# Fused attention and gated FFN on one core: another order of the opening, with the row sums of the first tiles folded before TensorE adds them

## The chip, the cores and the metric

The kernel runs on one core of a Trainium2 chip. The metric is the time of one execution in device microseconds (us); the median of three runs before the change is 1024.46 (1024.46 to 1024.63). Engines are named as in the profile: PE is TensorE, DVE is VectorE, ACT is ScalarE, POOL is GpSimd, SP is SyncE, which here only issues DMAs.

## What is computed

```python
B, C, Hh, Ww = 4, 128, 384, 32             # N = Hh*Ww = 12288 rows of q per image
kv_pool = kv.reshape(B, H//4, 4, W//4, 4, C).mean(axis=(2, 4))
k = v = kv_pool.reshape(B, -1, C) @ w_sr    # 768 keys per image
s = (q @ k.transpose(0, 2, 1)) / sqrt(C)
a = exp(s - s.max(-1)); a /= a.sum(-1)
x = (a @ v).reshape(B * N, C)               # 49152 rows
out = (maximum(x @ w_gate, 0) * (x @ w_val)) @ w_out    # d_ff = 1536
```

## The kernel before

The rows of q are cut into 96 tiles of 512. For a tile k the kernel makes the scores against 768 keys (six chunks of 128), exponentials, the product with the values (x, channels by rows), then twelve blocks of the FFN: v (value projection, L504), y (copy of v's bank to f16, L510), g (gate projection, L516), h (relu of the gate times the value, on DVE, L523), o (output projection, accumulated over the twelve, L545). The softmax's division is put off: the output is multiplied by the square of the inverse row sum, since the FFN is homogeneous of degree two in x.

Tiles 6 to 95 are worked by a loop over the fixed list STEADY (L106), one pass for each tile, in which four tiles overlap: scores of k, values of k-2, v, y, g, h of k-3, o of k-4. There ACT makes the exponentials with their row sums, and the weights' rows come transposed by DMA.

The change lies ahead of that loop, in the opening. A list of words, OPENING (L75), is walked once from left to right (L812); `open_step` (L678) issues for each word the instructions of one step. Every engine runs its instructions in the order in which they were issued, so the list is the order of each engine's queue; which engine takes a copy or an add is looked up by the word in ENGINES (L66: v DVE, a ACT, p POOL). "@n" names the PSUM bank (0 to 7) that the step's tile gets; the step then waits until the bank's last reader is done. Semaphores carry only dependences of data and of buffers.

The words, with the lines behind them:

- The twelve lines of the first image's kv (three pairs of chunks, four lines of pixels each, 512 KB a line, L229) and the first four tiles of q are loaded by SP and ACT (L641 to L646). Lines 0 to 3 of a pair hold the four rows of a 4x4 pooling window, for both chunks of the pair.
- a, b, c: adds of two lines, or of a line to the sum (L274); SUMS (L112) names the lines. p: sum of pixels 0, 1 with 2, 3 (L279); r: the last two pixels (L687). All are 128x512, 128x256, 128x128 in f32.
- T: transposes on PE, accumulated in one bank of chunk j: of a raw line (four pixels, four matmuls), or of a pixel sum ("p" two, "r" one) (L293). A raw line is thus added by PE instead of by an add. kvT: copy out of the bank; pj: product with w_sr; key: scaled copy to f16; vt, val: the same transposed, as values.
- cast, qt, qT: a tile of q to f16, its transpose on PE, the copy out of the bank. Tiles 4 and 5 come later: ql (L187) loads them, cast4 and cast5 run on POOL, qT4 and qT5 are DMA transposes on SP (L214).
- S k.j, E k.j, V k.j: scores, exponentials, values of tile k (0 to 3) and chunk j (L374, L380, L451). In these four tiles keys lie on the partitions, so ACT can't sum rows. xT k: copy of x out of its bank.
- U j...: the row sums of the four tiles over the chunks named: for each chunk four matmuls with 32 columns of ones, side by side in the array (L467). R: the sums transposed by DVE (L482); R2: inverse and square (L488); lsc: sixteen small copies of them on POOL (L493), used in the output of tiles 0 to 3.
- D, F: matmuls whose result nobody reads (L736, L670). The two of `fill(2)` (L667) stand ahead of the list.
- gate, W, wo, qd, qn, k: a tiny POOL copy that waits for a line of kv, then DMAs by POOL of the weights, and of q for later tiles.
- s, e of tiles 4 and 5, and oT (output transposed on DVE, scaled on POOL), as in the steady list.

Of the kernel before, what the change touches and what calls it, by code (L numbers as in the profile page):

```python
# [16 lines left out]
def kernel(  # L17
# [120 lines left out]
    def copy_on(name, to, what):
        engine = engine_of(name)
        if engine is nc.scalar:  # L140
            nc.scalar.copy(to, what)  # L141
        else:
# [765 lines left out]
```

## Time and profile before

| | us |
|---|---|
| median of three runs | 1024.46 |
| span of the profiled execution | 1022.5 |
| PE busy | 1017.2 |
| ACT busy | 918.5 |
| DVE busy | 869.4 |
| POOL busy | 524.0 |
| first v of the opening on PE | 27.74 |
| first word of the steady list on PE (v10 of tile 3) | 53.00 |

The span runs from the profiled execution's first instruction to its last; its own time as a run is not listed apart, and the runs' median lies 2.0 us above the span. Times in the timeline count from the span's start. A row of the timeline gives start, length and count of instructions merged into it; what stands in brackets is how long the engine was idle before, and whose end released it. A matmul's row includes the time that its result takes through the array, which overlaps the next one.

### The profile page before, as it was taken

The page shows a single profiled execution, that of the slowest core. Times are in us where ns is not written, and L with a number is a line of the kernel's source. Part 1 is how long each engine was busy: PE and PEld are TensorE (multiplying, and loading weights), DVE is VectorE, ACT ScalarE, POOL GpSimd, SP SyncE. Part 2 cuts the span into 40 slices and gives each one's busy share as a digit, 9 for nine tenths or more (in the row PEclk, how much of TensorE's full clock was granted, in tenths as well). Part 3 has the DMA queues.
Part 4 walks back from the last instruction along what each step waited for, and adds up shares of the span by engine and source line. Part 5 has one row for each costly group of instructions (what it writes and reads, how often), then busy time and mean ns, then how long its engine had stood idle before and what let it go on. Part 6 is the DMA issues. An engine that isn't in the chain of part 4 may idle for free.

```text
span 1022.5 us, 17480 instructions
## 1 busy us (share of the span) xinstructions
PE 1017.2 (99%) x5021; PEld 485.2 (47%) x5021; DVE 869.4 (85%) x1450; ACT 918.5 (90%) x1927; POOL 524.0 (51%) x1312
## 2 busy tenths in 40 slices
PE   9999999999999999999999999999999999999998
PEld 4444444444444444444444444444444444444445
DVE  5988888888888888888888888888888888888888
ACT  5999998999999999999999999999999999999986
POOL 3487857344437576544434856754434543443342
PEclk9999999999999999999999999999999999999999
DMA  9999999878799999868779999978787878777651
GB/s 317 172 171 184 186 211 145 140 122 132 132 198 156 201 164 184 136 116 143 125 134 201 165 186 187 157 131 137 128 130 114 147 122 129 124 119 124 98 91 44
DMA packets 475743, 153.48 MB, mean 150 GB/s; under 512 B 451584, under 2 KB 465920, under 8 KB 475648
## 3 DMA queue, kind: packets, MB, share of 16 engines
q1 hardware_dynamic: 453184, 126.08, 65.9%
q0 software_dynamic: 22032, 25.19, 17.6%
q10 hardware_dynamic: 432, 1.11, 0.3%
q8 instruction: 39, 0.64, 0.3%
q14 instruction: 56, 0.46, 0.2%
HBM read 53.94 MB, written 26.35 MB: 79 GB/s over the span
## 4 chain that ended last, share of the span: by engine, by line
PE 99%; DMA 1%; DVE 0%; ACTq 0%; issue 0%
PE bank_ps L504 24%; PE bank_ps L515 24%; PE bank_ps L545 24%; PE wide_ps L397 12%; PE bank_ps L439 12%; PE bank_ps L529 1%; DMA kv_in<-in_kv_dram 1%; PE bank_ps L456 1%; PE bank_ps L378 1%; PE wide_ps L336 0%; PE bank_ps L300 0%; PE bank_ps L314 0%; PE bank_ps L474 0%; DVE kv_s L272 0%; PE bank_ps L209 0%; ACTq L246 0%
## 5 line engine op out<-in xcount | busy, mean ns | idle before, releaser
L523 DVE SCALAR_TENSOR_TENSOR hT<-bank_ps,val 128x512 f16<-128x512 f32 x1152 | 727.3, 679 | 104.4 <-PE bank_ps L515 83.7
L141 ACT CAST val<-bank_ps 128x512 f16<-128x512 f32 x1149 | 628.4, 596 | 44.4 <-PE bank_ps L504 23.9
L504 PE MATMUL bank_ps<-xT,wv 128*128 128x512 f16 x1152 | 421.0, 379 | 0.0
L515 PE MATMUL bank_ps<-xT,wg 128*128 128x512 f16 x1152 | 376.3, 379 | 0.0
L545 PE MATMUL bank_ps<-hT,wo 128*128 128x512 f16 x1116 | 348.7, 379 | 0.0
L402 ACT ACTIVATE a<-wide_ps 128x768 f16<-128x768 f32 x368 | 302.2, 821 | 44.0 <-PE wide_ps L397 44.0
L397 PE MATMUL wide_ps<-kv,qT 128*128 128x512 f16 x736 | 179.8, 326 | 0.0
L439 PE MATMUL bank_ps<-aT,kv 128*128 128x512 f16 x552 | 179.0, 379 | 0.0
L558 POOL TENSOR_TENSOR o_sb<-o_t,scale 128x512 f32<-128x512 f32 x89 | 93.2, 1047 | 158.8 <-issue 141.0
L545 PEld LDWEIGHTS <-wo 128*128 128x128 f16 x1116 | 109.1, 98 | 132.1 <-issue 0.5
L515 PEld LDWEIGHTS <-wg 128*128 128x128 f16 x1152 | 112.6, 98 | 122.5 <-issue 0.2
L504 PEld LDWEIGHTS <-wv 128*128 128x128 f16 x1152 | 112.5, 98 | 105.4 <-issue 0.4
L423 POOL COPY scale<-square 32x8 f32<-32x8 f32 x736 | 141.2, 192 | 28.6
L416 POOL TENSOR_TENSOR square<-inverse 128x8 f32<-128x8 f32 x46 | 9.3, 202 | 248.9 <-DVE inverse L414 248.9
L838 POOL DMA_DIRECT2D out_dram<-o_sb x208 | 130.3, 632 | 9.6 <-POOL o_sb L558 7.4
L397 PEld LDWEIGHTS <-qT 128*128 128x128 f16 x736 | 71.9, 98 | 87.0 <-issue 0.2
L447 DVE CAST xT<-bank_ps 128x512 f16<-128x512 f32 x92 | 63.6, 691 | 31.7 <-PE bank_ps L439 31.6
L439 PEld LDWEIGHTS <-kv 128*128 128x128 f16 x552 | 53.9, 98 | 65.2
L402 ACT ACTIVATION_READ_ACCUMULATOR a<-wide_ps 128x1 f32 x368 | 76.1, 207 | 0.0
L553 DVE STREAM_TRANSPOSE o_t<-bank_ps 128x512 f32<-128x512 f32 x93 | 65.4, 703 | 0.3 <-PE bank_ps L504 0.2
L162 POOL DMA_DIRECT2D q<-in_q_dram x84 | 48.8, 581 | 0.3 <-issue 0.3
L256 POOL TENSOR_TENSOR s<-kv_in 128x512 f32<-128x512 f32 x36 | 45.1, 1281 | 0.7
(86 smaller groups left out, 210.8 us busy)
## 6 DMA issues: line engine op xcount, KB each, us to landing
kv_in<-in_kv_dram SPq DMA_DIRECT2D x42, 512.0 KB, 5.3
out_dram<-o_sb SPq DMA_DIRECT2D x177, 64.0 KB, 3.6
q<-in_q_dram POOLq DMA_DIRECT2D x88, 128.0 KB, 3.4
out_dram<-o_sb POOLq DMA_DIRECT2D x176, 64.0 KB, 4.2
aT<-a SPq DMA_TRANSPOSE x184, 4.5
kv_line<-in_kv_dram SPq DMA_DIRECT2D x4, 512.0 KB, 9.8
placed<-blocks SPq DMA_DIRECT2D x9, 128.0 KB, 2.5
kvT<-placed SPq DMA_DIRECT2D x36, 32.0 KB, 2.2
```

The source lines that it names most:

```text
L141: nc.scalar.copy(to, what)
L397: nc.tensor.matmul(s_ps[:, j0 * 128 : j1 * 128], qT, kv16[:, b, j0:j1, 0:C], start=True, stop=True)
L402: nc.scalar.activation(a16s[k][:, s, :], s_banks.pop(s)[:, 0:J], AF.Exp, scale=qk_scale, accum_out=a_sums[k // 2][:, k % 2, s : s + 1],)
L423: nc.gpsimd.tensor_copy(to[32 * b : 32 * (b + 1), :, :, j], squares[k // 2][32 * j : 32 * (j + 1)])
L439: nc.tensor.matmul(x_banks[k], kv16[:, k // NST, jc, C : 2 * C], aT[:, jc], start=first, stop=x_left[k] == 0,)
L504: nc.tensor.matmul(proj_banks["v", k, fb], wv16[:, fb * 128 : (fb + 1) * 128], xTs[k], start=True, stop=True,)
L515: nc.tensor.matmul(proj_banks["g", k, fb], wg16[:, fb * 128 : (fb + 1) * 128], xTs[k], start=True, stop=True,)
L523: nc.vector.scalar_tensor_tensor(hTs[k][:, fb, :], freed(proj_banks.pop(("g", k, fb))), 0.0, vals.pop((k, fb)), op0=ALU.max, op1=ALU.mult,)
L545: nc.tensor.matmul(o_banks[k], wo16[:, fb, :], hTs[k][:, fb, :], start=first, stop=o_left[k] == 0)
L553: nc.vector.transpose(o_t, freed(o_banks.pop(k)))
L558: nc.gpsimd.tensor_tensor(to, o_by, scale.to_broadcast([128, NS, 4, 32]), op=ALU.mult)
L838: queue.dma_start(*out_moves.pop())
```

## The change

- Each of the first six chunks now takes two line adds (lines 0 and 1, then 2), one pixel sum and one raw line: T j.3 and T j.p. Before, chunks 0, 2 and 5 turned two raw lines each, and chunks 1, 3 and 4 none.
- The row sums: new words m k.n add the exponentials of chunks 2n and 2n+1 of tile k, n k.1.2 adds the third sum to the second, so that chunks 0 and 1 lie in one f16 tile, chunks 2 to 5 in another. U6.7 then is the only sums step, over these two. Of the twelve m five are on DVE and seven on POOL; the four n are on POOL.
- D0, F384 and F256 go; D1 stays, in another place. `fill(2)` stays.
- The list and the engines are written anew. The gate of the weight loads waits for the same line (4.1 is line 1 of chunk 4), but stands behind m1.0 and m0.0 on POOL.
- The loads are named by a list; it gives the two queues the same transfers in the same order as before.

```diff
+    LOADS = """
+        p0l1:a p0l0 p0l3:a p0l2 w Q0 Q2 p1l0 p1l1 p1l2 p1l3 p2l0 p2l1 p2l2 p2l3
+    """.split()
-    SUMS = [{"a": [1, 0]}, {"a": [1, 0], "b": ["s", 3], "c": ["s", 2]}, {"a": [0, 1]}, {"a": [0, 1], "b": ["s", 2], "c": ["s", 3]}, {"a": [0, 1], "b": ["s", 2], "c": ["s", 3]}, {"a": [0, 1]}]
+    SUMS = [
+        {"a": [0, 1], "b": ["s", 2]},
...
+    ]
+    def pair_of(k, n):
+        if n not in a_pairs:
+            a_pairs[n] = work.tile(
+                [128, LEAD, T], FP16, tag="kv_s2" if n else "a_pair", bufs=2 if n else 1, name="a_pair"
+            )
+        return a_pairs[n][:, k]
+    def add_chunks(name, k, n):
+        add(name, pair_of(k, n), aTs[k][:, 2 * n], aTs[k][:, 2 * n + 1])
+    def add_pairs(name, k, n, m):
+        add(name, pair_of(k, n), pair_of(k, n), pair_of(k, m))
```

The engines and the list, before (-) and after (+), up to the first score blocks:

```diff
-        a0:v a1:v p0:v r0:v b1:v c1:v p1:v kvT0:v r1:p cast0:a cast1:a key0:v kvT1:v qT0:v
-        cast2:a cast3:v qT1:v val0:v key1:v qT2:v qT3:v val1:a a2:v a3:v p2:p b3:v c3:v kvT2:a
-        p3:p key2:a kvT3:a val2:v a5:v key3:v p5:v a4:v r5:v b4:v val3:a c4:v kvT5:a p4:v key5:v
-        kvT4:a val5:v key4:v val4:v xT0:v xT2:v y0.8:v y0.2:a xT1:v y2.0:a y0.10:a cast4:p y0.7:a
+        cast1:a a1:v a0:p b1:p b0:v cast0:a p0:v p1:p kvT0:a cast3:v kvT1:a qT1:v key0:v cast2:v
+        key1:v qT3:v qT0:a qT2:v val1:v a2:v val0:v b2:v p2:v a3:p kvT2:a b3:v p3:v kvT3:v key2:v
+        m3.0:v key3:v val2:v a5:v b5:v p5:v a4:v kvT5:a b4:v val3:a p4:v m1.0:p key5:v m0.0:p
+        m1.1:v m3.1:v kvT4:a val5:v key4:a m0.1:v val4:v m0.2:v xT0:v xT2:v xT1:v y0.10:a y0.2:a
+        y0.8:v y0.0:a y0.7:a y0.4:a m2.1:p m2.2:p y2.0:a m2.0:p m1.2:p y0.6:a cast4:p n2.1.2:p
+        y0.1:a cast5:p n0.1.2:p xT3:a y2.1:a y1.8:a y1.0:a m3.2:p n1.1.2:p y1.10:a y0.9:a n3.1.2:p
...
-        D1@2 D0@2 F384@2 a0 a1 p0 r0 T0.r@0 T0.3 b1 T0.2 c1 F256@2 p1 kvT0 r1 cast0 pj0@0 T1.r@1
-        cast1 qt0@2 key0 kvT1 vt0@0 qT0 qt1@3 cast2 pj1@1 cast3 S0.0@2 qT1 qt2@4 E0.0 qt3@5 val0
-        key1 qT3 S1.0@3 E1.0 vt1@1 val1 V0.0@2 S1.1@0 E1.1 S0.1@5 E0.1 qT2 S2.0@4 S2.1@1 V1.0@3
-        a2 S3.1@6 V1.1 E3.1 V0.1 S3.0@5 T2.2@0 V3.1@6 p2 E2.1 a3 T2.p V2.1@1 E2.0 b3 T2.3 c3 E3.0
-        U0.1@5 kvT2 pj2@0 V2.0 key2 p3 T3.p@4 kvT3 S2.2@0 E2.2 vt2@7 val2 V3.0 gate2.1 S1.2@4
-        E1.2 pj3@7 a5 S0.2@0 V2.2 W0 key3 W1 ql4 ql5 S3.2@4 E0.2 E3.2 p5 V1.2 a4 S3.3@7 S0.3@0
-        E3.3 V0.2 T5.2@4 E0.3 r5 T5.r vt3@7 val3 T5.3 kvT5 wo S1.3@0 S2.3@7 b4 c4 p4 V3.3 pj5@4
-        V3.2 E1.3 T4.p@0 E2.3 V1.3 key5 vt5@4 S2.5@7 kvT4 val5 pj4@0 key4 E2.5 S0.5@4 E0.5 V0.3
-        V2.3 S0.4@0 vt4@7 E0.4 V2.5 val4 S1.4@4 V0.5 E1.4 S2.4@7 V0.4 xT0 E2.4 S1.5@0 E1.5 S3.5@4
-        V1.4 V2.4 E3.5 S3.4@7 qd3 xT2 v0.8@2 v0.2@0 E3.4 qd1 V1.5 y0.8 v0.10@4 y0.2 v2.0@1 qd0
-        U2.3.4.5 xT1 y2.0 qd2 y0.10 cast4 v0.7@3 R v0.6@1 y0.7 g0.2@4 qT4 g2.0@0 h0.2 v0.0@2 y0.6
-        v2.1@3 cast5 g0.7@5 h2.0 V3.5 y0.0 g0.6@4 v0.1@1 qT5 h0.7 V3.4 y2.1 v1.10@2 g0.10@0 h0.6
-        xT3 o0.7@5 g0.1@3 y0.1 o0.2 h0.10 o0.6 y1.10 v0.5@4 h0.1 g0.0@1 g2.1@0 y0.5 v0.4@2 h0.0
-        o0.10 y0.4 v0.3@3 g0.4@4 h2.1 o0.0 y0.3 g1.10@2 v0.9@1 h0.4 g0.5@0 y0.9 v1.8@3 h1.10 s4.0
+        T0.3@2 cast1 a1 a0 b1 b0 cast0 T1.3@5 p0 p1 D1@6 T0.p kvT0 cast3 qt1@0 T1.p kvT1 qt0@3
+        pj0@1 qT1 key0 qt3@4 pj1@2 cast2 key1 S1.0@6 qt2@5 qT3 S1.1@7 S3.1@1 qT0 S3.0@0 qT2 vt1@3
+        vt0@2 S2.1@4 E1.0 val1 E1.1 S0.0@6 a2 E3.1 S2.0@5 V3.1@7 V1.1@1 S0.1@3 E2.1 val0 b2 E3.0
+        V1.0 p2 E2.0 V2.1@2 a3 V3.0 V2.0 T2.p@4 E0.0 E0.1 T2.3 kvT2 T3.3@0 b3 p3 T3.p pj2@5 kvT3
+        key2 m3.0 V0.0@6 pj3@3 S1.2@0 V0.1 vt2@4 key3 val2 E1.2 S3.2@5 a5 S2.2@3 S0.3@4 b5 p5 V1.2
+        S0.2@0 E3.2 E2.2 V3.2 E0.2 S1.3@5 V2.2 E1.3 S3.3@3 V0.2 E3.3 a4 T5.p@0 T5.3 vt3@3 kvT5
+        S2.3@5 pj5@0 b4 val3 T4.3@3 E0.3 p4 m1.0 T4.p key5 m0.0 m1.1 m3.1 S2.5@4 E2.3 kvT4 vt5@0
+        S0.5@5 val5 gate4.1 E2.5 pj4@3 W0 V3.3 V2.3 key4 m0.1 V2.5 E0.5 W1 ql4 S0.4@3 vt4@0 S2.4@4
+        ql5 S1.5@5 val4 E0.4 E2.4 V0.5 wo S1.4@0 V0.3 E1.5 E1.4 V0.4 S3.4@3 qd1 qd2 m0.2 V2.4
+        S3.5@4 V1.5 V1.3 E3.4 V1.4 E3.5 xT0 v0.10@5 v0.8@6 xT2 v0.2@0 g0.10@3 xT1 y0.10 y0.2 g0.2@2
+        v0.0@4 v2.0@1 qd3 v0.7@5 g0.7@0 y0.8 qd0 h0.10 v0.4@6 y0.0 V3.4 g0.0@4 y0.7 v0.6@3 h0.2
+        y0.4 g2.0@5 V3.5 g0.6@2 m2.1 h0.7 v0.1@6 m2.2 y2.0 h0.0 m2.0 v2.1@0 m1.2 g0.1@1 v1.8@4 y0.6
+        o0.7@3 cast4 n2.1.2 h2.0 o0.0 y0.1 v1.10@6 cast5 n0.1.2 xT3 g0.4@5 h0.6 g2.1@7 v1.0@2 y2.1
+        o0.10 y1.8 y1.0 o0.2 g1.8@0 h0.1 h0.4 m3.2 v0.9@1 qT4 g0.5@4 h2.1 n1.1.2 y1.10 y0.9 h1.8
+        v0.5@5 g1.10@2 qT5 s4.0 o0.4 v0.3@1 o0.1 g0.9@0 n3.1.2 h1.10 o0.6 v1.11@2 y0.5 e4.0 g0.8@5
+        h0.5 y0.3 s4.1 y1.11 U6.7@4 h0.9 h0.8 v1.1@1 e4.1 R g0.3@0 v2.3@2 o0.9 y1.1 h0.3 y2.3
...
```

More of the change, by code (lines that the diff above doesn't have):

```diff
@@ L471, in lead_sums @@
                 x_banks["sums"] = bank([128, T])
-            sums_left[0] -= 1
             for k in range(LEAD):
                 nc.tensor.matmul(
-                    x_banks["sums"][32 * k : 32 * (k + 1), :], ones, aTs[k][:, jc, :],
-                    start=first, stop=sums_left[0] == 0, skip_group_check=True,
+                    x_banks["sums"][32 * k : 32 * (k + 1), :], ones,
+                    aTs[k][:, jc, :] if jc < NJC else pair_of(k, jc - NJC),
+                    start=first, stop=last and jc == chunks[-1], skip_group_check=True,
                     tile_position=(0, 32 * k),
```

86 lines of the change are left out of this document (54 added, 32 removed).

## The prediction, made before the changed kernel was run

> **What bounds the kernel now.** I read the page first (totals, then the chain that ended last), then busy time by windows, then the timeline of the first 56 us, engine by engine. The text names steps by the words of the order lists: E2.5 is tile 2's exponential over chunk 5, S, V, T, v, y, g, h, o, U, m, n likewise, k.x meaning tile k.
>
> ```profile
> span 1022.5 us, 17480 instructions
> PE 1017.2 (99%) x5021; PEld 485.2 (47%) x5021; DVE 869.4 (85%) x1450; ACT 918.5 (90%) x1927; POOL 524.0 (51%) x1312
> ...
> PE 99%; DMA 1%; DVE 0%; ACTq 0%; issue 0%
> ```
>
> TensorE is the chain to the end. The edit touches only the opening list, so the question is when the first word of the steady list (v10, the 37th value projection) reaches TensorE; everything behind it keeps its length, if the engines hand over in the same state.
>
> ```profile
> 27.74 0.59 PE L504 MATMUL bank_ps<-xT,wv 128*128 128x512 f16 x2
> ...
> 28.91 1.05 PE L474 MATMUL bank_ps<-aT,ones 128*32 128x512 f16 x16
> ...
> 36.17 0.49 PE L397 MATMUL wide_ps<-kv,qT 128*128 128x512 f16 x2
> ...
> 53.00 0.38 PE L504 MATMUL bank_ps<-xT,wv 128*128 128x512 f16 x1
> ```
>
> The opening's first projection starts at 27.74, the steady list at 53.00. In the chain of waits a projection counts for what it adds, not for its row's 0.38:
>
> ```profile
> 27.91 0.43 PE bank_ps L504 x2
> ```
>
> That is 0.216 each; a score block (the 0.49 of 36.17, less the same tail of 0.16) adds 0.33. The profiled execution's time is the span 1022.5 plus 2.0 around it, which is the median 1024.46; so a change of the 53.00 goes straight into the median.
>
> ```profile
> 5.00:8.50 3.50, 3.37 (x8) 1.17 (x7) 1.94 (x5) 0.00 (x0) 0.00 (x0) 1.00 1.03 415
> ...
> 12.40:27.70 15.30, 15.30 (x97) 8.14 (x95) 10.02 (x23) 13.27 (x30) 7.46 (x14) 1.00 1.06 302
> ...
> 30.70:53.00 22.30, 22.30 (x108) 10.32 (x106) 22.18 (x40) 21.55 (x47) 12.11 (x34) 1.00 0.94 161
> ```
>
> Columns: stretch, length, busy time of PE, PEld, DVE, ACT, POOL, granted clock, DMA share, GB/s. Until 12.4 DMA is full and the engines wait for data. From 12.4 to 27.7 ACT is the fullest engine (24 exponentials and copies). From 30.7 to 53 PE, DVE (22.18 of 22.30) and ACT (21.55) are all full: a balanced stage, in which none of the three has room.
>
> **Part 1, loads.** The new load list gives each queue the same transfers in the same order; cost nothing. This fixes the end of the exponentials:
>
> ```profile
> 19.22 0.19 POOL L747 COPY gate<-kv_line 128x1 f32<-128x1 f32 x1 [0.96 <-DMA kv_line<-in_kv_dram]
> ...
> 21.28 0.42 PEld L300 LDWEIGHTS bank_ps<-ident,kv_line 128*128 128x128 f32 x4 [0.33 <-ACT aT L381]
> ...
> 22.59 0.27 ACT L141 COPY kvT_chunk<-bank_ps 128x128 f32<-128x128 f32 x1 [0.18 <-PE bank_ps L300]
> ...
> 23.98 0.27 ACT L141 COPY kvT_chunk<-bank_ps 128x128 f32<-128x128 f32 x1
> ...
> 24.41 4.32 ACT L381 ACTIVATE aT<-bank_ps 128x512 f16<-128x512 f32 x8 [0.17 <-PE bank_ps L378]
> ...
> 28.58 3.54 ACT L141 CAST val<-bank_ps 128x512 f16<-128x512 f32 x6
> ```
>
> POOL's gate waits for line 1 of the last pair, 19.2. Two more lines of 512 KB at the 415 GB/s of the first window (1.26 us each) come at 20.5 and 21.7 by estimate. The eight exponentials of chunks 4 and 5 (0.52 us each with their gaps, 24.41 to 28.58) can't start until the last line is transposed, copied, projected and kept. No order of the list moves that by more than some tenths.
>
> **Part 2, the start.** Chunks 0 and 1 now take two line adds each (a1, b0 on DVE, a0, b1 on POOL), a pixel sum and one raw line, and the fillers go. What sets the first exponential is not the sums but the copies of q:
>
> ```profile
> 10.23 1.90 ACT L141 CAST q<-q 128x512 f16<-128x512 f32 x3 [6.57 <-DMA q<-in_q_dram]
> ...
> 11.89 0.42 DVE L143 CAST q<-q 128x512 f16<-128x512 f32 x1
> ...
> 12.28 0.61 PE L209 MATMUL bank_ps<-ident,q 128*128 128x128 f16 x8
> ...
> 12.48 1.26 ACT L381 ACTIVATE aT<-bank_ps 128x512 f16<-128x512 f32 x2 [0.35 <-PE bank_ps L378]
> ...
> 13.78 3.12 ACT L381 ACTIVATE aT<-bank_ps 128x512 f16<-128x512 f32 x6
> ...
> 17.34 0.27 ACT L141 COPY kvT_chunk<-bank_ps 128x128 f32<-128x128 f32 x1 [0.45 <-PE bank_ps L300]
> ...
> 19.07 3.14 ACT L381 ACTIVATE aT<-bank_ps 128x512 f16<-128x512 f32 x6
> ```
>
> Now E1.0 stands on ACT behind qT0 and qT2. qT2 needs qt2, which needs cast2; cast2 stands on DVE behind cast3, qT1 and key0. q's second pair has landed by 11.5 (the third cast on ACT ended at 12.1 and takes 0.6). So 11.5 + cast3 0.4 + qT1 0.35 + key0 0.3 + cast2 0.35 + turn on PE 0.45 + qT2 0.45 = 13.8 for E1.0, against 12.48: 1.3 us later. The sums themselves can run side by side and still hide: kvT0 stands on ACT behind two casts until 11.3. Six raw lines take 24 turns on PE and the pixel sums 12, 36 against 33, in a stage where PE waits anyway.
>
> **Part 3, chunks 2 to 5.** With eight exponentials behind 13.8 (0.5 each, 3.12 for six) ACT is free at 17.8 for kvT2, which started at 17.34; E1.2 comes at about 19.3 against 19.07. Six exponentials then end at 22.4, before kvT5 can start (22.6). On DVE key5 now stands behind b5, p5, a4, b4, p4 (20.5 + 0.7 + 0.4 + 0.7 + 0.7 + 0.4 = 23.4), no later than its projection lets it. kvT4 24.05, E2.5 24.3, key4 takes 0.25 on ACT, then six more exponentials: first y at 28.5 against 28.58. Five of the adds m are on DVE (m1.1 and m3.1 ahead of val5, which V2.5 and, behind it on PE, S0.4 wait for).
>
> ```profile
> L272 DVE TENSOR_TENSOR kv_s<-kv_in 128x512 f32<-128x512 f32 x4 | 2.6, 688 | 5.8 <-DMA kv_in<-in_kv_dram 5.8
> L143 DVE CAST q<-q 128x512 f16<-128x512 f32 x1 | 0.4, 416 | 0.0
> ```
>
> An add of two f16 tiles of 512 is not in the trace. Bounds: 0.42 (one input) and 0.69 (two inputs, f32). At 0.42 it costs nothing, at 0.69 S0.4 comes 0.3 late. I take 0.1.
>
> The Trainium skill (VectorE: DVE Perf Modes, Mode 2x_1P) lets a two-input operation on dense 16-bit tiles give two results a cycle. By estimate from that page's clock the add would take 0.27 us and a start, and the 0.1 would go; no row of this trace has such an operation.
>
> So TensorE's first projection: 27.74 + 0.25 = 28.0 (it stands on PE behind V1.4, which needs E1.4, the third last exponential: begun at 27.0, done 0.6 later).
>
> **Part 4, the row sums.** Before, six steps of four 32-column matmuls; four of these steps stand behind the first projection and take 0.98 (16 starts, to 29.89). Now two steps, all behind it: 0.5 less on PE. One V less stands there too (0.22). PE from the first projection to the steady list: 25.26 - 0.5 - 0.22 = 24.55. 28.0 + 24.55 = 52.55, if nothing waits. On DVE:
>
> ```profile
> 30.75 9.08 DVE L523 SCALAR_TENSOR_TENSOR hT<-bank_ps,val 128x512 f16<-128x512 f32 x15
> ...
> 54.10 1.97 DVE L523 SCALAR_TENSOR_TENSOR hT<-bank_ps,val 128x512 f16<-128x512 f32 x3
> ```
>
> DVE runs without a gap from 30.75 to 55.4 (24.6 us). Now xT0 comes at 26.9 (V0.4 behind E0.4), then xT2, xT1, y0.8 at 0.6 each (9.08 for 15), and the first h at 29.3, since no sums step stands between the v's and the g's; one y leaves DVE (-0.6), the turning of the sums comes into the stretch (+0.7). It would end at 54.0. ACT takes one y more (0.5), out of the 0.75 that it idles between 30.7 and 53: no cost, but no room.
>
> What pays for the two removed thirds of the steps is POOL: seven m and four n.
>
> ```profile
> L558 POOL TENSOR_TENSOR o_sb<-o_t,scale 128x512 f32<-128x512 f32 x89 | 93.2, 1047 | 158.8 <-issue 141.0 <-DVE o_t L553 14.5 <-DMA aT<-a 3.3
> L256 POOL TENSOR_TENSOR s<-kv_in 128x512 f32<-128x512 f32 x36 | 45.1, 1281 | 0.7
> L143 POOL CAST q<-q_late 128x512 f16<-128x512 f32 x2 | 1.2, 609 | 6.4 <-DMA q_late<-in_q_dram 6.4
> ...
> 14.91 1.04 POOL L272 TENSOR_TENSOR kv_c<-kv_s 128x256 f32<-128x256 f32 x1 [4.01 <-PE bank_ps L378]
> ...
> 15.42 1.08 DVE L272 TENSOR_TENSOR kv_s<-kv_s,kv_in 128x512 f32<-128x512 f32 x1
> ...
> 17.54 0.72 POOL L272 TENSOR_TENSOR kv_c<-kv_s 128x256 f32<-128x256 f32 x1 [1.58 <-DVE kv_s L272]
> ...
> 22.72 2.19 POOL L758 DMA_DIRECT2D q<-in_q_dram x4
> ...
> qT<-q SPq DMA_TRANSPOSE x3, 2.5
> ```
>
> An f16 add on POOL is not shown either. Bounds: 0.61 (the cast, one input) and 1.83, which is 1.28 times 1.04/0.72, the stretch of a POOL add that ran beside a DVE add of two SBUF tiles. I take 1.25, the f32 add, since it ran at that price beside DVE's h. m1.0 and m0.0 now stand before the gate of the weight loads; m0.0 needs E0.1 (17.8) and ends at 19.1, just in time for 19.2. POOL's DMA issues end at 24.9 as before; m2.1 fits in; m2.2 waits for E2.4 (26.7). Then eight adds and two casts: 26.7 + 8 x 1.25 + 1.2 = 37.9. PE comes to U6.7 after 17 v, 14 g, 7 o, 2 V (0.216 each) and two score blocks (0.33): 9.3, so 37.3. It waits 0.6, and DVE's turn of the sums, with all h behind it, 1.0, which its earlier start covers. The casts of q for tiles 4 and 5 are in that queue; cast4 at 30.5, its transpose lands 2.5 later (last row above), 33.6; s4.0 comes behind 15 v, 12 g, 4 o, 2 V at 35.3: hidden by 1.7 us, at 1.83 an add gone.
>
> **The sum.** 28.0 + 24.55 + 0.6 = 53.15, less 0.1 to 0.2 of the gaps around the old sums step: 53.0. That is no change: 1024.5.
>
> **Rivals.**
>
> (a) *Forecast*: gains at the sums steps and at DVE are eaten by the later start and the wait at U6.7. 1023.6 to 1025.6. Chance 0.52.
>
> (b) *Slower: POOL's adds arrive late at U6.7.* TensorE is in order, and so is DVE behind R; nothing else fills. At 1.83 an add: 26.7 + 14.6 + 1.2 = 42.5, a wait of 5.2 in place of 0.6, 1029. It passes 0.2% from 1.5 us an add. For it: POOL works 13 us on end with no slack, and any slip at its gate moves the weight loads too. Against: L256 kept 1.28 in 36 cases. Chance 0.18.
>
> (c) *Clock.* Without D0 and the fills, PE idles from the end of the two fills to the landing of line 3:
>
> ```profile
> 1.37 3.78 PE L663 MATMUL bank_ps<-ident 128*128 128x512 f32 x4 [1.37 <-POOL ident masks.py:199]
> ...
> 5.01 2.46 PE L738 MATMUL bank_ps<-kv_in,ident 128*128 128x512 f32 x4
> ...
> 8.51 1.09 PE L300 MATMUL bank_ps<-ident,kv_in 128*128 128x128 f32 x8
> ```
>
> That is 5.15 to 8.5, where the windows have 3.37 of 3.50 busy today at clock 1.00. The first fills took 0.95 each, the next ones of their size 0.6. If PE ran so slowly again from 8.8 to about 12.2, its 8 turns, D1 and the projections (3 us) would take 1.5 longer; E1.0 comes 1.2 later, half of that is swallowed by the wait for the last line, the rest and later weights stay: 1025.5, at most 1027. Chance 0.18, a third of it past 0.2%. The Trainium skill (TensorE: Matmul & The Clock Gate, What's actually happening) has the clock halved after an idle window of about 3.4 us; by it an idle stretch of 3.3 us stands on the edge, and no idle stretch in this trace tests it.
>
> (d) *Faster*: adds at 1.05 or less, no wait at U6.7, DVE's lead of 1.4 us lets PE run dense, first projection at 27.7: 28.0 - 0.3 + 24.55 = 52.25, 1023.7; with DVE ahead by its 1.4 at the steady list's start, the first steady tiles may give some of that too, 1022.3 to 1023.5. PE's own sum has no 2 us. Chance 0.12, half of it past 0.2%.
>
> **Numbers.** 0.2% (2 us) is about what a measurement of this kernel can tell from no change. Same: (a) 0.52, two thirds of (c) 0.12, half of (d) 0.06: 0.70. Slower: (b) 0.18 and a third of (c) 0.06: 0.24. Faster: 0.06. The range leaves out (b) and ends at (c)'s likely worst and below (d): 1022.2 to 1026.6; (a)'s own is 1023.6 to 1025.6.
>
> **What would show it.** In the profile after: E1.0 near 13.8; first y near 28.5; first L504 near 28.0; POOL's adds 1.25 each, the last n ending near 38; a gap of about 0.6 on PE before the eight tiled matmuls; first h near 29.3; the 37th L504 at 53.0; clock 1.00 in the windows. Wrong if the first y moves by over 1 us, if s4.0 or the g's wait for a DMA, or if the part behind the 37th L504 is no longer 969.5 us (1022.5 - 53.0).

## The result, and the profile after

The changed kernel takes 1028.90 us (median of five runs, 1028.17 to 1031.77), the one before 1024.63 beside it (1024.46 to 1026.49): 1.0048 times as long, 95% interval 1.0035 to 1.0062. It is slower, where no change was forecast. The changed kernel's runs spread over 3.6 us, and the profiled execution is the longest of them.

The first reading is TensorE's timeline, the rows that carried the forecast's sum (start, length, what ran, count):

```profile
span 1030.0 us, 17458 instructions
```

```profile
32.66 0.81 PE L532 MATMUL bank_ps<-xT,wv 128*128 128x512 f16 x3
...
42.04 0.61 PE L501 MATMUL bank_ps<-a_pair,ones 128*32 128x512 f16 x8
...
57.06 0.38 PE L532 MATMUL bank_ps<-xT,wv 128*128 128x512 f16 x1
```

The first projection (L532 is L504 of before) starts at 32.66, the steady list at 57.06. So the span of 1030.0 splits like this against before and forecast:

| | first projection, start | from there to the 37th | behind the 37th | span |
|---|---|---|---|---|
| before | 27.74 | 25.26 | 969.46 | 1022.5 |
| forecast | 28.0 | 25.0 | 969.5 | 1022.5 |
| after | 32.66 | 24.40 | 972.93 | 1030.0 |

The stage with the folded row sums (from the first projection to the 37th) gained 0.86 against before. Everything was lost on its two sides: 4.9 ahead of it, 3.5 behind it. Two views show where to look. Busy time by windows (length; PE, PEld, DVE, ACT, POOL; clock; DMA share; GB/s), and what PE waited for (total, times, longest):

```profile
5.00:8.50 3.50, 0.00 (x0) 0.00 (x0) 0.69 (x1) 0.00 (x0) 1.77 (x1) 0.90 1.03 414
8.50:12.40 3.90, 3.83 (x12) 2.69 (x13) 2.49 (x3) 1.14 (x2) 2.57 (x2) 0.50 1.03 421
12.40:15.00 2.60, 2.60 (x21) 2.37 (x19) 0.90 (x3) 1.12 (x3) 0.76 (x1) 0.57 1.02 406
```

```profile
PE bank_ps L315 <- DMA kv_in<-in_kv_dram: 3.7, 1, 3.7
PE bank_ps L454 <- DMA aT<-a: 2.2, 1, 2.2
```

PE is idle for 3.7 us, up to 8.57. Its granted clock is 0.50 from 7.82 to 14.65 (the profile records each change), and PE is busy nearly all the time from 8.57 on (3.83 of 3.90). The second wait stands in a steady tile, for the transposed exponentials:

```profile
118.29 0.38 PE L454 MATMUL bank_ps<-aT,kv 128*128 128x512 f16 x1 [2.18 <-DMA aT<-a]
```

On ACT, the first exponential (E1.0), kvT2, the second set (E1.2) and the first y were 12.48, 17.34, 19.07 and 28.58 before, and 13.8, 17.8, 19.3 and 28.5 in the forecast:

```profile
15.38 0.60 ACT L396 ACTIVATE aT<-bank_ps 128x512 f16<-128x512 f32 x1 [0.81 <-PE bank_ps L393]
...
21.04 0.27 ACT L153 COPY kvT_chunk<-bank_ps 128x128 f32<-128x128 f32 x1 [1.00 <-PE bank_ps L315]
23.65 3.04 ACT L396 ACTIVATE aT<-bank_ps 128x512 f16<-128x512 f32 x6 [2.35 <-PE bank_ps L393]
...
33.09 3.12 ACT L153 CAST val<-bank_ps 128x512 f16<-128x512 f32 x6
```

1.6 are lost by the first exponential, 3.2 by kvT2, 4.35 by E1.2, hardly more behind it. What lies between is DVE's and POOL's, where adds of two SBUF tiles meet:

```profile
9.68 1.37 DVE L287 TENSOR_TENSOR kv_c<-kv_s 128x256 f32<-128x256 f32 x1
...
14.73 1.07 DVE L155 CAST q<-q 128x512 f16<-128x512 f32 x1
...
17.22 1.66 DVE L287 TENSOR_TENSOR kv_s<-kv_in 128x512 f32<-128x512 f32 x1
...
20.70 1.26 DVE L287 TENSOR_TENSOR kv_c<-kv_s 128x256 f32<-128x256 f32 x1
...
22.97 0.41 DVE L287 TENSOR_TENSOR a_pair<-aT 128x512 f16<-128x512 f16 x1
...
24.06 0.68 DVE L287 TENSOR_TENSOR kv_s<-kv_line 128x512 f32<-128x512 f32 x1
```

```profile
8.99 1.78 POOL L287 TENSOR_TENSOR kv_s<-kv_s,kv_in 128x512 f32<-128x512 f32 x1 [0.79 <-DMA kv_in<-in_kv_dram]
...
14.24 1.27 POOL L287 TENSOR_TENSOR kv_s<-kv_in 128x512 f32<-128x512 f32 x1 [2.61 <-DMA kv_in<-in_kv_dram]
17.18 1.15 POOL L287 TENSOR_TENSOR a_pair<-aT 128x512 f16<-128x512 f16 x1 [1.67 <-ACT aT L396]
20.11 1.56 POOL L287 TENSOR_TENSOR a_pair<-aT 128x512 f16<-128x512 f16 x1 [1.79 <-ACT aT L396]
21.63 0.38 POOL L791 COPY gate<-kv_line 128x1 f32<-128x1 f32 x1
```

a2 takes 1.66 beside m1.0 and p3 1.26 beside m0.0; the same operations take 0.68 and 0.42 a little later in the same queue. An f16 add alone on DVE takes 0.41, as at 22.97. The first meeting stands in chunks 0 and 1: p0, a pixel sum like p3, takes 1.37 at 9.68 beside POOL's b1, which takes 1.78 itself. Nor is it adds alone: the cast of a tile of q at 14.73 (cast2, one input, from SBUF to SBUF) takes 1.07 beside POOL's a3, where the cast at 11.60 took 0.43. And POOL's gate, with the weight loads behind it, moves from 19.2 to 21.6. Last, POOL behind the opening:

```profile
58.28 1.07 POOL L174 DMA_DIRECT2D q<-in_q_dram  x2 [10.18 <-DMA qT<-q]
59.41 1.05 POOL L586 TENSOR_TENSOR o_sb<-o_t,lead_scale 128x512 f32<-128x512 f32 x1
```

The loads of k5 wait 10.18 for a turn of q to be done (tq1: it frees the buffer that k5 loads into; it stood right behind g0.8 and 47 words ahead of k5, and now stands 63 words behind g0.8 and 9 ahead of k5), and the first scaling of outputs waits behind them, until 59.4.

### The profile page after: what moved, and what is told of

Same layout as the page of the kernel before. It is cut to its first block, busy times and chain, and to the rows that moved or that the text cites. A ratio compares the mean times of both kernels' runs of the same rounds, so it can differ in the third digit from the quotient of the medians.

```text
span 1030.0 us, 17458 instructions
## 1 busy us (share of the span) xinstructions
PE 1016.8 (99%) x5002; PEld 486.7 (47%) x5002; DVE 873.1 (85%) x1450; ACT 918.4 (89%) x1928; POOL 540.3 (52%) x1324
## 4 chain that ended last, share of the span: by engine, by line
PE 96%; DMA 2%; DVE 1%; ACT 0%; issue 0%; SPq 0%; ACTq 0%
PE bank_ps L532 24%; PE bank_ps L543 23%; PE bank_ps L573 23%; PE bank_ps L454 12%; PE wide_ps L412 11%; DMA aT<-a 1%; PE bank_ps L557 1%; DMA kv_in<-in_kv_dram 1%; DMA qT<-q 1%; PE bank_ps L315 0%; PE bank_ps L393 0%; PE bank_ps L471 0%; PE wide_ps L351 0%; ACT val L153 0%; PE bank_ps L329 0%
## 5 line engine op out<-in xcount | busy, mean ns | idle before, releaser
L532 PE MATMUL bank_ps<-xT,wv 128*128 128x512 f16 x1152 | 420.5, 379 | 0.0
L532 PEld LDWEIGHTS <-wv 128*128 128x128 f16 x1152 | 112.7, 98 | 105.6 <-issue 0.8
```

Source lines behind the costliest of these rows:

```text
L532: nc.tensor.matmul(proj_banks["v", k, fb], wv16[:, fb * 128 : (fb + 1) * 128], xTs[k], start=True, stop=True,)
```

## The experiments

Four losses could be read from these lines: the clock; the meeting of POOL's and DVE's adds; the late tq1; and what the new order of DVE and TensorE costs by itself. All kernels compute the same function as the two compared; fillers, whose results nobody reads, come and go, and the row sums are folded or not. The last four columns are read from one profiled execution of each kernel, as in the table above ("stage" is from the first projection to the 37th, "behind" what follows); the ratio is to the kernel before, run beside it.

| run | median us | ratio, 95% interval | first projection | stage | behind | span |
|---|---|---|---|---|---|---|
| e1_fill | 1028.24 | 1.0042 [1.0026, 1.0058] | 30.83 | 24.40 | 970.12 | 1025.3 |
| e2_tq | 1027.44 | 1.0031 [1.0021, 1.0041] | 32.72 | 24.40 | 969.98 | 1027.1 |
| e3_sums6 | 1027.37 | 1.0027 [1.0018, 1.0037] | 29.09 | 25.27 | 969.16 | 1023.5 |
| e4_before_nofill | 1026.22 | 1.0014 [1.0005, 1.0023] | 29.67 | 25.26 | 969.47 | 1024.4 |
| e5_fill_tq_sums6 | 1025.31 | 1.0009 [1.0000, 1.0018] | 28.94 | 25.26 | 969.20 | 1023.4 |
| e6_late_m | 1028.67 | 1.0047 [1.0034, 1.0059] | 32.47 | 24.40 | 969.99 | 1026.9 |
| e7_reorder | 1029.87 | 1.0050 [1.0036, 1.0064] | 34.18 | 24.41 | 969.17 | 1027.8 |
| e8_mixed | 1028.51 | 1.0038 [1.0026, 1.0051] | 32.31 | 24.93 | 969.18 | 1026.4 |
| e9_apart | 1024.93 | 1.0005 [0.9997, 1.0014] | 29.16 | 24.40 | 969.42 | 1023.0 |
| e10_old_apart | 1024.07 | 0.9997 [0.9989, 1.0006] | 28.34 | 24.52 | 969.66 | 1022.5 |
| e11_letters | 1031.04 | 1.0067 [1.0049, 1.0084] | 30.02 | 24.40 | 976.40 | 1030.8 |
| e12_a3 | 1025.18 | 1.0007 [0.9998, 1.0016] | 29.00 | 24.40 | 969.67 | 1023.1 |
| e13_pj2 | 1025.75 | 1.0012 [1.0003, 1.0021] | 29.46 | 24.40 | 969.65 | 1023.5 |
| e14_pj2_a3 | 1024.81 | 1.0002 [0.9993, 1.0012] | 29.38 | 24.40 | 969.17 | 1023.0 |
| e15_a5 | 1024.98 | 1.0004 [0.9995, 1.0013] | 28.75 | 24.40 | 970.12 | 1023.3 |

### One part at a time

**e1: the fillers back**

```diff
-        T0.3@2 cast1 a1 a0 b1 b0
+        D1@2 D0@2 F384@2 T0.3@2 cast1 a1 a0 b1 b0
```

> The changed kernel with the three fillers D1, D0 and F384 put back at the head of its list, nothing else. Clock theory (PE idles from 4.85 to 8.57, falls to half clock until 14.65, and all later lateness follows from that): granted clock stays 1.00, E1.0 at 13.8 instead of 15.4, first v near 28.3 instead of 32.66, time about 4 us below the changed kernel's 1028.9, near 1025. Queue theory (DVE's new order and POOL's adds beside DVE's make chunks 2 to 5 late by themselves): clock 1.00 and E1.0 near 13.8 too, but the first v still at 30.5 or later, time 1027 or more.

The clock is at 1.00 where it was 0.50, and the first projection comes 1.83 sooner: that is the price of the clock between these two profiles. The medians lie only 0.66 apart, with runs from 1027.14 to 1031.10: the late tq1 is still there. 3.1 of the loss ahead of the first projection stayed, as the queue theory had it, and DVE shows where (a2, val0, b2, p2):

```profile
8.50:12.40 3.90, 3.84 (x26) 2.54 (x27) 2.83 (x4) 1.65 (x5) 2.57 (x2) 1.00 1.03 419
```

```profile
14.71 1.33 DVE L287 TENSOR_TENSOR kv_s<-kv_in 128x512 f32<-128x512 f32 x1
15.96 0.21 DVE L155 COPY kv<-bank_ps 128x128 f16<-128x128 f16 x1
16.09 1.50 DVE L287 TENSOR_TENSOR kv_s<-kv_s,kv_in 128x512 f32<-128x512 f32 x1
17.63 1.40 DVE L287 TENSOR_TENSOR kv_c<-kv_s 128x256 f32<-128x256 f32 x1
```

b2 and p2 are 1.8 longer than their 0.68 and 0.42. This profile also shows what E1.0 stands behind on ACT: qT0, but no qT2, which is on DVE (the second of the two turns from 13.40 on, 13.77 to 14.20) and comes after E1.0 has begun:

```profile
12.38 0.59 ACT L153 COPY qT<-bank_ps 128x512 f16<-128x512 f16 x1
13.43 4.09 ACT L396 ACTIVATE aT<-bank_ps 128x512 f16<-128x512 f32 x8 [0.47 <-PE bank_ps L393]
```

```profile
13.40 0.80 DVE L155 COPY qT<-bank_ps 128x512 f16<-128x512 f16 x2
```

**e2: tq1 early**

```diff
-        g0.8@5 h0.5
+        g0.8@5 tq1 h0.5
-        o1.4 tq1 h1.6
+        o1.4 h1.6
```

> The changed kernel with the word tq1 (the DMA transpose that frees the q buffer for which the loads of k5 wait) moved forward to g0.8, as it stood in the kernel before. Transfer theory: POOL no longer stands 10 us before the k5 loads, no wait for aT near 118, the part behind the 37th v goes back from 972.9 to about 969.5-970.0; 37th v still at 57; time about 2.5 us below 1028.9, near 1026.3. If that stand is covered: part behind stays near 972.9, no change.

k5's loads go out at 48.1 with no wait ahead of them:

```profile
48.12 1.08 POOL L174 DMA_DIRECT2D q<-in_q_dram  x2
50.85 1.05 POOL L586 TENSOR_TENSOR o_sb<-o_t,lead_scale 128x512 f32<-128x512 f32 x1 [1.65 <-DVE o_t L581]
```

The part behind the 37th projection is 969.98, 2.95 less than in the changed kernel, and the wait at 118 is gone. The first projection didn't move. So the late tq1 is a loss of its own; e1, which kept it, lost nothing there in its profile (970.12), so it doesn't cost the same each time. The time fell by less than expected, by 1.5 at the median to 1027.44.

**e3: without the folded sums**

```diff
-        m1.0 m0.0 m1.1 m3.1
...
-        n3.1.2
...
-        U6.7@4
+        U0.1.2.3.4.5@4
```

> The changed kernel without the adds m and n: one sums step over the six chunks in the place of the step over two folded sums. Queue theory, with its part on POOL's adds: a2 and p3 on DVE fall back to 0.69 and 0.42, E1.2 about 1.5 us earlier, first v near 31; then four more groups on PE (1 us) in the stage from the first v, so the 37th v 0.5 to 1 us earlier than 57.06. Clock theory: first v unchanged at 32.5, 37th v about 0.9 later, at 58.

All sixteen m and n are out. a2 took 1.13, p2 and p3 0.43 and 0.42, the first projection came 3.6 sooner, and the stage, with the sums step, took 0.87 more. Both theories had the first projection later. But the half clock, too, lasted only from 7.77 to 11.19 in that profile, so this run alone doesn't price the adds.

**e4: the kernel before, without its fillers**

```diff
-        D1@2 D0@2 F384@2 a0 a1 p0 r0 T0.r@0 T0.3 b1 T0.2 c1 F256@2 p1
+        a0 a1 p0 r0 T0.r@0 T0.3 b1 T0.2 c1 p1
```

> The kernel before without its fillers D1, D0, F384, F256, nothing else. Clock theory: half clock from 7.8 to about 14.6, first E 1.5 us later or more, first v 2 us later or more, time 1026.5 or more. If the old order has slack for it (its exponentials end on the last line's landing at 21.7): half clock, but first v at most 0.7 later than 27.74, time within 1 us of 1024.5.

In this profile, where the clock is at 0.50 from 8.06 to 14.88, the fillers are worth 1.9 us at the kernel before's first projection:

```profile
8.10:14.80 6.70, 5.67 (x31) 4.80 (x32) 4.49 (x13) 2.25 (x4) 0.46 (x1) 0.50 1.04 415
```

Not every execution pays that. Of the ten runs three took 1024.61 to 1024.69, no longer than the kernel before, with a mean granted clock of 0.998; five took 1025.83 to 1026.34 at 0.997, as the profiled one; the other two, 1026.64 and 1026.78, have no kept trace that would explain them. By estimate a stretch of 3.41 us at half clock, as in e3, takes the mean to 0.998, and one of 6.83, as here, to 0.997. So the opening has slack for the shorter stretch and none for the longer.

### All at once, and the adds moved

**e5: fillers, early tq1, no folded sums**

```diff
+        D1@2 D0@2 F384@2
...
+        tq1
-        U6.7@4
+        U0.1.2.3.4.5@4
```

(The edits of e1, e2 and e3 together.)

> The changed kernel with three things at once: the fillers D1, D0 and F384 ahead of the list, tile 1's write and turn (tq1) moved up to right behind g0.8, and no adds m and n (the sums step takes the six chunks one by one). If the three losses are separate (clock 1.8, POOL's adds beside DVE's about 2, the late loads of k5 up to 3) they add: first value projection at 28.6 to 29.0, stage to the 37th 25.3 (four more groups of sums), 37th at about 54.1, the rest 969.5, time 1025.3 and the same from run to run within 1. If the losses are one and the same (all come from the clock), this one stands where the first experiment stood, first projection near 30.8, 1027 or more.

Met on every number: the losses add up. What remains of the new order itself is 1.2 at the first projection.

**e6: the folded sums back, POOL's two early adds later**

```diff
-        p4 m1.0 T4.p key5 m0.0 m1.1 m3.1
+        p4 T4.p key5 m1.1 m3.1
-        g0.6@2 m2.1 h0.7
+        g0.6@2 m1.0 m0.0 m2.1 h0.7
```

(With the edits of e1 and e2, as all that follow but e11.)

> As the run before, but with the adds m and n kept; only m1.0 and m0.0, POOL's two f16 adds that stand before its gate, are put behind its loads, just ahead of m2.1. If it is these two adds that hold up DVE's a2, b2 and p2: a2 0.7 to 1.1, b2 0.7, p2 0.43, kvT2 at 18.3, first projection 28.6 to 29.0, stage 24.4, 37th at 53.1 to 53.6, time 1024.4 to 1025.0. If the adds are innocent and the order of the list alone is late: p2 still over 1.2, first projection at 30.8, time 1026.5. If the two moved adds are then late for the sums step: a wait of up to 2.5 ahead of the tiled matmuls.

Missed by 4 us, and the most telling run of all. DVE and POOL from 25.3 on:

```profile
25.40 3.79 DVE L287 TENSOR_TENSOR a_pair<-aT 128x512 f16<-128x512 f16 x2
29.11 0.21 DVE L155 COPY kv<-bank_ps 128x128 f16<-128x128 f16 x1
29.25 0.41 DVE L287 TENSOR_TENSOR a_pair<-aT 128x512 f16<-128x512 f16 x1
```

```profile
25.30 3.61 POOL L287 TENSOR_TENSOR a_pair<-aT 128x512 f16<-128x512 f16 x3
```

```profile
PE bank_ps L471 <- DVE kv L155: 2.6, 2, 2.3
```

p2 and p3 were back at 0.43, but the moved adds now stood beside m1.1 and m3.1 on DVE: two adds of 0.41 took 3.79, about as long as POOL's three. Singly, DVE's ended at 27.90 and 29.19, each 0.3 behind the end of one of POOL's (27.61 and 28.91). val5 behind them kept TensorE for 2.3. The meeting was moved, not removed. One row stays unexplained: p4, just ahead of these adds, took 1.27 in place of 0.43 (in e7 too), while POOL was only issuing loads.

**e7: e6 with another order on DVE**

```diff
-        a3:p
+        a3:v
...
-        qT3 S1.1@7
+        qT3 a2 S1.1@7
...
-        S0.0@6 a2 E3.1
+        S0.0@6 E3.1
...
-        key2 m3.0 V0.0@6
+        key2 V0.0@6
...
-        key5 m1.1 m3.1
+        key5 m3.0 m1.1 m3.1
```

(On e6.)

> The kernel of the run before with DVE's order mended as well: a2 ahead of val1, a3 on DVE in place of POOL, m3.0 behind key5. If the remaining lateness of the first projection against the forecast (28.0) is DVE's order, it comes at 28.0 to 28.4, the 37th at 52.4 to 53.0, time 1023.8 to 1024.5. If the start is bound elsewhere (the last line's landing, ACT's exponentials), the first projection stays at 28.7 to 29.0 and the time at that of the run before, within 0.3.

The same meeting, now of three adds with three (3.80 on DVE), and behind TensorE's wait of 2.3 its clock halved, from 29.92 to 33.34:

```profile
27.00:29.90 2.90, 0.61 (x4) 0.26 (x4) 2.68 (x4) 0.48 (x1) 1.93 (x2) 1.00 1.48 229
29.95:33.30 3.35, 3.35 (x11) 1.15 (x9) 1.27 (x3) 2.37 (x5) 2.08 (x2) 0.50 0.89 230
```

It says nothing on DVE's order.

**e8: the old opening with the new sums**

```diff
+        key4 m3.0 m1.1 m3.1
...
+        val4 m0.1 m0.2
...
+        g0.6@2 m1.0 m0.0 m2.1
```

(The opening of the kernel before, with its SUMS, engines and fillers, up to the first projection; from there the new list.)

> The old opening up to the first value projection (with its engines, sums, fillers and load gate), then the new list with the folded row sums, m1.0 and m0.0 on POOL behind the loads, m3.0, m1.1, m3.1, m0.1, m0.2 on DVE behind key4 and val4, and tq1 right behind g0.8. If the row sums are a gain by themselves and only the opening of the change loses: first projection at 27.7 to 28.1, stage 24.4, 37th at 52.2 to 52.6, the rest 969.5, time 1023.6 to 1024.1, below the kernel before. If the folded sums gain nothing once the opening is right (POOL late at the sums step, or DVE short of the 1.3 us that its five adds take): a wait of 0.5 to 1.5 ahead of the tiled matmuls, 37th at 53 or later, 1024.5 or more.

Again the meeting (4.12 for three adds on DVE from 25.1), behind it a wait of TensorE of 3.0, and again a halved clock, from 29.95 to 33.36; 1.05 of that lie in the stage, which took 24.93 in place of 24.40. Neither alternative was tested.

### The adds kept apart in time

**e9: the new list with the adds m apart**

```diff
+        p3 m3.0 m1.0
...
+        key5 m1.1
...
+        val5 m3.1 m0.1 m0.0
...
+        val4 m2.1 m2.0
...
+        g0.6@2 m2.2 h0.7
...
+        m1.2 m0.2 g0.1@1
...
+        h0.4 m3.2
```

(The first eight on DVE, the last four on POOL.)

> The new list with fillers and the early tq1 again, but the twelve adds m dealt out so that no add of two SBUF tiles on DVE stands beside one on POOL: m3.0, m1.0 behind p3, m1.1 behind key5, m3.1, m0.1, m0.0 behind val5, m2.1, m2.0 behind val4, all on DVE, where it waited in the kernel without m and n; m2.2, m1.2, m0.2, m3.2 and the four n on POOL behind its loads. If it is the pairing of the two engines that costs: each DVE add 0.41, first projection 28.9 to 29.2, stage 24.4, 37th 53.3 to 53.6, time 1024.4 to 1024.8. If an f16 add is dear on DVE wherever it stands (rival): m beyond 1 us each, first projection past 31, time 1027 or more.

Met, but for the time, 0.13 above what was expected. Three of the adds in a row on DVE, with POOL idle beside them (it waits from 25.15 to 27.88), and POOL's own, with DVE on copies and h, which read PSUM:

```profile
25.37 1.09 DVE L287 TENSOR_TENSOR a_pair<-aT 128x512 f16<-128x512 f16 x3
```

```profile
27.88 3.38 POOL L287 TENSOR_TENSOR a_pair<-aT 128x512 f16<-128x512 f16 x3 [2.73 <-ACT aT L396]
```

Three f16 adds take 1.09 where three took 3.80 in e7, so the rival, a dear f16 add, is out. The 3.7 us between e6 and e9 are the engines and places of the adds, nothing else. DVE's line adds from 20.6 to 24.2 and m1.1 at 24.51 took their own 0.68, 0.43 and 0.41 while POOL issued loads.

**e10: the old opening, with the adds apart**

```diff
+        c3 p3 E3.0 m3.0 m1.0 m0.0 m2.0 kvT2
...
+        key5 m1.1
...
+        val5 m3.1
...
+        val4 m0.1 m0.2 m2.1
```

(On e8; p3 on DVE in place of POOL; m2.2, m1.2 and m3.2 on POOL, placed as in e9.)

> The old opening with the new sums, the adds dealt out in the same way: p3 on DVE, m3.0, m1.0, m0.0, m2.0 behind it, m1.1 behind key5, m3.1 behind val5, m0.1, m0.2, m2.1 behind val4, all on DVE; m2.2, m1.2, m3.2 and the four n on POOL. If the row sums are a gain of 0.86 once the adds stand apart: first projection 27.7 to 28.1, 37th 52.2 to 52.6, the rest 969.3, time 1023.5 to 1024.0, below the kernel before by 0.4 to 0.9. If nine adds on DVE (3.3 us of it) come back as a later first projection: 28.6 or more, 53.0 or more, 1024.4 or more.

In between: 1024.07, 0.3 below the kernel before at its median, which the interval can't tell from it. The first projection is 0.6 later than before, where 0.27 is a later landing of the loads in that execution (POOL's gate at 19.49 against 19.22); the rest, 0.33, would be what nine adds and p3 on DVE cost, which no run shows by itself. The stage gives 0.74 back. Four of the nine, in a row:

```profile
18.11 1.43 DVE L280 TENSOR_TENSOR a_pair<-aT 128x512 f16<-128x512 f16 x4
```

**e11: the changed kernel, two letters**

```diff
-        p4:v m1.0:p key5:v m0.0:p
+        p4:v m1.0:v key5:v m0.0:v
```

> The changed kernel with two letters changed: m1.0 and m0.0 on DVE (where they stand, behind p4 and key5) in place of POOL. No fillers, tq1 late as in the change. If POOL's two adds hold up a2, b2, p2, p3: these take 0.7 to 1.3, 0.7, 0.43, 0.43; DVE pays 0.75 for the two adds; POOL's gate comes 2 us sooner; first projection 30.2 to 31.2 against 32.66, time 1026.3 to 1028 depending on what k5's loads lose. If the stretch is not theirs: first projection at 33 or later, 1029 or more.

The first half came as expected, or a little better: a2 0.68, p2 and p3 0.42, the gate at 19.2, the first projection at 30.02 (2.6 sooner, of which some is the clock: it was at half only from 9.23 to 12.64 here). The second half didn't. What PE waited for, and the windows from 110 on:

```profile
PE bank_ps L454 <- DMA aT<-a: 4.2, 1, 4.2
PE bank_ps L315 <- DMA kv_in<-in_kv_dram: 3.4, 1, 3.4
```

```profile
110.00:115.00 5.00, 3.00 (x15) 1.19 (x13) 3.78 (x6) 3.24 (x7) 1.66 (x3) 1.00 1.20 213
115.20:121.80 6.60, 4.56 (x12) 1.73 (x13) 1.38 (x2) 1.49 (x3) 5.41 (x7) 0.50 1.17 225
```

With tq1 still late, the steady tile waited 4.2 for its transpose (113.0 to 117.24), and the clock halved within that wait, from 115.04 to 121.87: 976.40 behind the 37th, 7 us gone. A start that is 2.6 sooner did not make the kernel faster. Its six runs go from 1028.35 to 1034.40, those of the changed kernel from 1028.17 to 1031.77, and the intervals of the two ratios overlap.

### What remains of the new order

e9 starts the projections at 29.16, where the forecast had 28.0.

**e12: e9 with a3 on DVE**

```diff
-        a3:p
+        a3:v
```

> The kernel e9_apart with one letter more: a3, POOL's last add of lines, on DVE (behind p2). It stood beside DVE's a2, which took 1.35 there. If the rest of the late start against the forecast (29.16 against 28.0) comes from that meeting: a2 0.69, p2 ends 0.65 sooner, kvT2 at 17.7, the second set of exponentials at 19.5, first projection at 28.5 to 28.7, 37th 52.9 to 53.1, time 1024.2 to 1024.5. If chunk 3's fold, 0.69 later on DVE, takes it back, or the order on PE sets kvT2: first projection 29.1 or later, time 1024.9 or more.

kvT2 did come at 17.58 (18.38 in e9, 0.26 of it from an earlier landing) and a2 took 0.68, but E1.2 stayed at 19.99 (20.14):

```profile
17.58 0.27 ACT L153 COPY kvT_chunk<-bank_ps 128x128 f32<-128x128 f32 x1
19.99 3.04 ACT L396 ACTIVATE aT<-bank_ps 128x512 f16<-128x512 f32 x6 [2.15 <-PE bank_ps L393]
```

ACT now waits 2.15 for the score block that E1.2 reads: chunk 2's projection (pj2) stands on TensorE behind the turn of chunk 3's pixel sum.

**e13 and e14: pj2 ahead of that turn, in e14 with a3 on DVE**

```diff
-        b3 p3 m3.0 m1.0 T3.p pj2@5 kvT3 key2 V0.0@6 pj3@3 S1.2@0 V0.1 vt2@4 key3 val2
+        b3 p3 pj2@5 key2 T3.p kvT3 m3.0 S1.2@5 V0.0@6 pj3@3 V0.1 vt2@4 key3 m1.0 val2
```

> The kernel e9_apart with chunk 2's projection and key (pj2, key2) ahead of chunk 3's last turn (T3.p), its first score block ahead of V0.0 in a bank that key2 itself frees (banks 0 and 5 swapped from there to S1.4), m3.0 behind kvT3 and m1.0 behind key3. If the place of pj2 behind T3.p sets E1.2: E1.2 at about 1.1 behind kvT2, 19.5 in place of 20.14, first projection 28.5, 37th 52.9, time 1024.2 to 1024.4. If it doesn't: E1.2 at 20.1, first projection 29.1, 1024.9.

> The same with a3 on DVE behind p2, where it alone gained 0.16 of 0.65 in the run before. If pj2's place was what took the rest: kvT2 17.6, E1.2 18.8 to 19.2, first projection 28.0 as in the forecast (or held at 28.2 by the last line's landing), 37th 52.4 to 52.7, time 1023.8 to 1024.2. If a3 on DVE now delays kvT3 and S3.2: E1.2 early but a gap behind it, first projection 28.6 or more, 1024.4 or more.

E1.2 came at 19.75 and 19.51, 0.2 to 0.6 sooner than in e9 and e12; the first projection came later, at 29.46 and 29.38. In e13 the exponential behind E1.2 waited for its own block, and a5 on DVE stood at 20.86, against 20.56 in e9:

```profile
19.75 0.60 ACT L396 ACTIVATE aT<-bank_ps 128x512 f16<-128x512 f32 x1 [1.35 <-PE bank_ps L393]
20.68 2.75 ACT L396 ACTIVATE aT<-bank_ps 128x512 f16<-128x512 f32 x5 [0.33 <-PE bank_ps L393]
```

In nine profiles of the new list (after, e1, e2, e3, e5, e9, e12, e13 and e14, with a5 from 20.3 to 24.1) the first projection stands 8.60 behind a5, the first add of the last pair's lines; in after, whose row of a5 is above, 32.66 - 24.06. (In e6, e7 and e11 a meeting of adds ahead of val5 comes between: 11.69, 13.38 and 9.45.) a5 stands behind val2.

**e15: e9 with a5 earlier**

```diff
-        key2 V0.0@6 ... key3 val2 E1.2 S3.2@5 a5
+        key2 a5 V0.0@6 ... key3 val2 E1.2 S3.2@5
```

> The kernel e9_apart with one word moved: a5 behind key2, ahead of key3 and val2, where DVE waits 0.58 for TensorE. If DVE's chain of the last pair (a5, b5, p5, a4, b4, p4, key5) sets the first projection: b5 at 20.7 in place of 21.27, first projection 28.5 to 28.7, 37th 52.9 to 53.1, time 1024.2 to 1024.5. If ACT or the landing of the last line sets it: first projection still at 29.1, 1024.9; if key3 and val2, 0.1 to 0.3 later, are what counts: 29.3 or more.

b5 came at 20.44, 0.83 sooner, of which 0.34 is an earlier landing of the loads in that execution (POOL's gate at 19.12 against 19.46). The first projection at 28.75 is 0.41 sooner, so the edit itself gave less than 0.1: key5 now waited 0.51 for TensorE, and kvT5 stood on ACT right behind the six exponentials from E1.2 on. So two chains, ACT's from E1.2 and DVE's from a5, seem to lie within 0.1 of each other, and each of the last runs brought one of them forward. That moving both would bring 28.0 was not tried. By the medians none of e12 to e15 is more than 0.12 below e9. Nor was p0 kept from b1 in any run of the new list; its E1.0 is no later than forecast, but what that meeting costs is not shown.

## Why the prediction was wrong, step by step

- **What fails first**: "The sums themselves can run side by side and still hide", and with it Part 3's walk. In chunks 0 and 1 the cost did hide (Part 2 below); behind them it did not. The prediction took DVE's and POOL's adds at their own durations. The quoted rows had the price (1.08 against 0.69 on DVE, 1.04 against 0.72 on POOL) and Part 4 used it only for the length of POOL's adds, never for a2, p2 and p3 beside m1.0 and m0.0. It is worth 1.7 at the first projection (e1 30.83, e9 29.16) as the change has it, and 3.3 where the adds meet in front of val5 (e6 32.47, e9 29.16). The Trainium skill states it (SBUF — State Buffer, Who interferes with whom): a DVE instruction with two inputs in SBUF contends with a GpSimd instruction that reads SBUF, and the one that comes second is blocked, not slowed. The rows of e6 agree: each of DVE's two adds of 0.41 ends 0.3 behind the end of one of POOL's, the first after two of them.
- **The clock (rival c)** was right in kind and a size too small: "half of that is swallowed by the wait for the last line". PE idled 3.7, the half clock lasted to 14.65, E1.0 came at 15.38 in place of 13.8, and 1.83 reached the first projection (e1). Nothing was swallowed: the path to the first projection runs over kvT2, val2 and a5, all late by then, not over the landing of the last line. By the Trainium skill (TensorE: Matmul & The Clock Gate, What's actually happening) an idle window of about 3.4 us halves the clock and a busy one sets it free, on windows that run on whatever the kernel does. The traces agree: all recorded changes of the clock lie whole multiples of 3.41 apart. In after the window from 4.41 to 7.82 was busy for 0.13 of its length, and the clock halved at its end; 7.82 to 11.24 was busy for 0.78 and did not set it free; 11.24 to 14.65 was busy throughout and did. In e3, with 3.6 idle, 7.77 to 11.19 was busy for 0.80, which was enough, and E1.0 came at 13.70. So the same idle time can cost one window of half clock or two, which the rival's single price could not hold. In e2 the record has no full clock before 13.65: there it had not been granted yet.
- **"Everything behind it keeps its length"** failed: 972.93 against 969.5. The step that I never priced is tq1, now 63 words behind g0.8, and k5's loads, which need the buffer that it frees. e2 gives 2.95 for it, e11 lost 6.9 behind the 37th with it.
- **Part 2** had the right time by the wrong path: E1.0 came at 13.3 to 13.8 in the runs with fillers and the new opening (13.8 forecast). But the sum of casts and turns that gave 13.8 ends in "E1.0 stands on ACT behind qT0 and qT2", and qT2 is on DVE in the new list. In e1 it ran from 13.77 to 14.20, when E1.0 had begun at 13.43, behind qT0 and a wait of 0.47 for TensorE. That the number held was luck.
- **Part 3, the order**: with fillers and the adds apart, kvT2 18.38 (17.8), E1.2 20.14 (19.3), E2.5 25.17 (24.3), first projection 29.16 (28.0). "On DVE key5 now stands behind b5, p5, a4, b4, p4 (20.5 + ...)" had a5 end at 20.5; it started at 20.56, behind val2, which itself waited for TensorE, and ended at 21.24. So both walks of Part 3, ACT's and DVE's, were 0.8 to 0.9 short; which step of the new order takes the 1.2 between 28.0 and 29.16 stays open, since neither moving a3 and pj2 nor moving a5 brought it back. The f16 add at 0.42 was right.
- **Part 4** was right in its sum: stage 24.40 without a wait (24.55 forecast), POOL's f16 add 1.15 where nothing stood beside it (1.25). The wait of 0.6 at U6.7 was not put to the test: in e9 the last n ends at 37.9, as forecast, but PE comes there at 38.5, 1.2 later than forecast. One step of it failed: m0.0 "just in time" for the gate; it ended at 21.6, and the weight loads went out at 21.95, 2.6 later than before. Rival (b), POOL's adds late at U6.7, wasn't the cause.
- The sum, against before: 1.83 of clock (after to e1), 1.7 of meeting adds (e1 to e9) and 1.4 of the new order (e9 to before; 0.25 of it was forecast) are the 4.92 ahead; 0.86 back in the stage; 2.95 of 3.47 behind it from tq1. The other 0.5 behind is within what the profiles differ by (969.2 to 970.1), and the loads land up to 0.3 sooner or later from one execution to the next.

## What to carry to other kernels

When work goes to POOL to relieve TensorE, look at what DVE does at that moment: in these runs an add of two SBUF tiles on each made DVE's wait for the end of POOL's, and moving POOL's add made it worse (e6). Put such adds on one engine, or where the other reads PSUM or idles. When a list is reordered, walk also the words that compute nothing (a buffer's last reader, a load behind it, a filler): two of the four losses here lie in those, and each was undone by moving or restoring a few words. And when a forecast names a path, look up on which engine each of its steps stands: a number that comes out right doesn't show that the path was.
